# A new order of the work around the first scan of a gated mix of two state space layers

## The chip, the core and the metric

The kernel runs on one core of a Trainium2 chip. The metric is the time of one execution on the device in microseconds (us), and of several executions the median. The engines are named as in the profile: PE is TensorE's matmul, PEld its weight load, DVE is VectorE, ACT is ScalarE, POOL is GpSimd and SP is SyncE. SPq and POOLq are their queues of transfers.

## The reference

Two layers work on the same x (2048 steps, 1024 channels, bf16), and a gate mixes them:

```python
g = sigmoid((x * gate_w).sum(-1, keepdims=True))
# a: a diagonal complex state space layer with 1024 states
Bu = x @ B_bar.T
h[t] = Lam_bar * h[t-1] + Bu[t]
a = 2 * Re(h @ C.T) + x * Dskip
# b: a causal convolution of 2048 taps in each channel, by its spectrum
k_shift = sum(k[t - i] * shift_k[:, i] for i in range(4))
kv = k_shift * v
y = causal_conv(kv, ssm_k) + kv * ssm_D
b = x * y
out = g * a + (1 - g) * b
```

## The kernel before

The work has two stages, and both give TensorE much to do.

**The convolution** goes through eight chunks of 128 channels (`c` from 0 to 7, the loop over `range(NC - 1)` in the lower half of the kernel). For a chunk TensorE makes the four taps of k as products with diagonals (`taps`), the spectrum of the kernel rows (`fwd_K`, PSUM tile `psk`), a mirrored copy (`mirror`), the spectrum of k times v (`fwd_V`, `psv`), and the way back (`inverse`, `psz` and `low`). VectorE multiplies the spectra. `mid_products` is a generator for chunks 1 to 6: it is called piece by piece (`step`) between other work, up to each `yield`. Its products go to `G` and to `T2` (a part of the tile BT[2]), with `WK` and two rotating tiles `t` as rooms; some sums are done by accumulating transfers that POOL issues (`gather`). `overlap` prepares two rows of kernel spectra (`KR`, and the second half of K in place). For even chunks the spectrum of the kernel lies in BT[3], the tile into which the last part of B is loaded after chunk 6. While the loop works on the products of chunk c, it already prepares chunk c + 1 (`n`) and loads c + 2 (`nn`).

**The state space layer** splits time into four blocks `tb` of 512 steps and the states into four groups `g` of 256; 16 pairs (tb, g). `Bu` gives half a pair's product with B at a time (16 matmuls into one PSUM tile `bu`, copied by ScalarE to `U`); these halves are laid out by hand, as fillers, through the convolution and the scans. `scan` treats one pair: the odd steps by VectorE's scan instruction, with turns by a table of sines (`turned`, tiles P and R); the even steps come from the odd ones (`by_lam` on ScalarE makes Q, `evens` adds it to U). `ahead` makes the same for the odd steps (R). `advance(i)` makes `ahead` for one or two later pairs, runs the function `between`, and then scans pair i with the finishing of output row i - 5 (`finish`).

An output row block is 128 steps by 1024 channels. `Cy(tb, tl)` multiplies the states of the four groups by C (32 matmuls, 8 for a group, PSUM tile `psy`), and `scale_a` copies it with the gate to `ga`. `scale_b` scales the convolution's row `pbb` on ScalarE and adds x's skip term by a transfer. `loads` fetches a row of the convolution from DRAM (`cv_scr`, where `inverse` leaves it through `stores`) and one of x; the last four rows (12 to 15) are put into the tiles BT[0] and BT[1], where B's first two groups were. `turn_C` and `part_C` multiply C by complex factors, on VectorE and ScalarE by turns.

What sets the order: every engine takes its instructions in the order in which the Python code issues them (`put` chains them per engine), so the order of the calls is the schedule. PSUM has four tiles of two banks, handed out in rotation (`ps2`): a matmul group waits until the copy of the group four allocations earlier is done. SP issues nearly all loads and stores, in order; POOL issues the accumulating transfers.

Of the kernel before, what the change touches and what calls it, by code (L numbers as in the profile page):

```python
# [9 lines left out]
ALU = mybir.AluOpType  # L10
# [10 lines left out]
def kernel(  # L21
# [40 lines left out]
    NG = NP // 2  # L62
# [29 lines left out]
    def ps2(shape, name):  # L92
        return psum.tile(shape, F32, name=name, tag="ps")
# [17 lines left out]
    def step(gen):  # L111
        next(gen, None)

    def run(gen):
        for _ in gen:
            pass
# [5 lines left out]
    def tt(o, a, b, op):  # L122
        put("dve", V.tensor_tensor, out=o, in0=a, in1=b, op=op)
# [325 lines left out]

    nC = {}  # L450

    def part_C(pi):

        n = nC[pi] = n4([128, 2, D], BF16, "n")
        for c in range(2):
            if pi % 2:
                act(n[:, c], CT[pi][:, 1 - c], func=ACT.Identity, scale=mc2i[:, pi:pi + 1])
            else:
                ts(n[:, c], CT[pi][:, 1 - c], mc2i[:, pi:pi + 1], None, ALU.mult)

    def turn_C(pi):

        if pi % 2 == 0:
            part_C(pi)
        n = nC.pop(pi).rearrange("p c d -> p (c d)")
        for c, f in enumerate((c2r, mc2r)):
            ts(CT[pi][:, c], CT[pi][:, c], f[:, pi:pi + 1], None, ALU.mult)
        o = CT[pi].rearrange("p c d -> p (c d)")
        if pi % 2:
            tt(o, o, n, ALU.add)  # L470
        else:
            gather(o, n)
# [101 lines left out]
    def kr_of(K, h):  # L574

        w = K.shape[3]
        return KR[:, h * 768:h * 768 + 3 * w].rearrange("p (b x) -> p b x", x=w)

    def overlap(c, h=0):

        K = KH[c][h].rearrange("p c b f d -> p c b (f d)")
        tt(kr_of(K, h), K[:, 0, 1:4], K[:, 1, 0:3], ALU.add)
        tt(K[:, 1, 1:4], K[:, 1, 1:4], K[:, 0, 0:3], ALU.subtract)

    def fwd_V(c, fis=range(NFI)):
        eo = eos["v", c]
# [63 lines left out]
    def mid_products(c):  # L650

        GH[c] = spectrum("G", c)
        K, Vt, G = (x[c][0].rearrange("p c b f d -> p c b (f d)") for x in (KH, VH, GH))
        w = 512
        T2 = BT[2].rearrange("p c d q -> p (c d q)")

        def mult(a, k, room):
            t = room.rearrange("p (c b x) -> p c b x", c=2, x=w) if room is not G else G
            ka = kr_of(K, 0)[:, None, a - 1:a] if a and not k else K[:, k:k + 1, a:a + 1]
            tt(t, bc(ka, [128, 2, 4 - a, w]), Vt[:, :, 0:4 - a], ALU.mult)  # L660
            return t

        mult(0, 0, G)
        yield
        gather(G[:, :, 1:], mult(1, 0, WK[:, 0]))
        yield
        t2 = mult(0, 1, T2)
        gather(t2[:, :, 1:], mult(1, 1, WK[:, 1]))
        yield
        i2 = mult(2, 1, u4([128, 4 * w], BF16, "t"))  # L670
        i3 = mult(3, 1, u4([128, 2 * w], BF16, "t"))
        tt(i2[:, :, 1:], i2[:, :, 1:], i3, ALU.add)
        yield
        r2_ = mult(2, 0, WK[:, 0, 0:4 * w])
        r3 = mult(3, 0, WK[:, 0, 4 * w:])
        tt(r2_[:, :, 1:], r2_[:, :, 1:], r3, ALU.add)
        yield
        tt(G[:, :, 2:], G[:, :, 2:], r2_, ALU.add)
        yield
        tt(t2[:, :, 2:], t2[:, :, 2:], i2, ALU.add)  # L680
        tt(G[:, 0], G[:, 0], t2[:, 1], ALU.subtract)
        tt(G[:, 1], G[:, 1], t2[:, 0], ALU.add)

# [75 lines left out]
    def Bu(n=1):  # L759
        steps(Bu_halves, int(2 * n))  # L760
# [131 lines left out]
    def Cy_g(tb, tl, ps, g, last, by_half=False):  # L892
        t0 = HP + tl * 128
        tsl = slice(t0, t0 + 128)
        order = [(j, c, dh) for j in range(2) for c in range(2) for dh in range(2)]
        for j, c, dh in sorted(order, key=lambda o: o[2]) if by_half else order:
            mm(ps[dh], hbs[tb, g][:, c, j, tsl], CT[2 * g + j][:, c, dh * 512:(dh + 1) * 512],
               g == 0 and j == 0 and c == 0, last and j == 1 and c == 1)
# [6 lines left out]
    def scale_a(t_, ps):  # L905
# [2 lines left out]
            act(ga[:, o], i, func=ACT.Identity, scale=gcols[:, t_:t_ + 1])  # L908
        gas[t_] = ga

    def Cy(tb, tl):
        ps = ps2([128, 2, 512], "psy")
        for g in range(NG):
            Cy_g(tb, tl, [ps[:, 0], ps[:, 1]], g, g == NG - 1)
        scale_a(tb * 4 + tl, [(slice(0, D), flat(ps))])

    def finish(t_, ps=None):
# [71 lines left out]
    prod = none  # L989
    for c in range(NC - 1):  # L990
        n, nn = c + 1, c + 2
        if c == 0:
            load("kT", nn)
            load_BT(c, 0)
            load_BT(c, 1)
            load_xT(0)
            load("v", 2)
            load("kn", nn)
            p1 = products(0, 1, by_dma=False)
            step(sp)  # L1000
            fwd_K(n, (0, 1))
            step(p0)
            run(tv)
            overlap(0, 1)
            step(p1)
            step(sp)
            step(p1)
            step(p0)
            step(p1)
            run(p0)  # L1010
            taps(nn, dg)
            load("kT", nn + 1)
            fwd_K(n, (2, 3))
            step(p1)
            step(sp)
            fwd_V(n)
            run(turns)
            dg = dgs(nn + 1)
            run(p1)
            tv = times_v(nn)  # L1020
            step(tv)
            add_skip(nn)
            Bu()
            step(tv)
            taps(nn + 1, dg)
            overlap(n)
            step(sp)
            continue
        tabs, back, last, prod = turn_table(c - 1, u4), inverse(c - 1), prod, mid_products(c)
        if nn + 1 < NC:  # L1030
            load("kT", nn + 1)
        if c == 1:
            load_BT(c, 0)
            load_BT(c, 1)
        if c == 2:
            load_xT(1)
        step(prod)
        run(tv)
        step(prod)
        run(last)  # L1040
        if nn < NC:
            if c > 1:
                taps(nn, dg)
            load("kn", nn)
            tv = times_v(nn)
            step(tv)
        if nn + 1 < NC:
            dg = dgs(nn + 1)
        fwd_K(n)
        if nn + 1 < NC:  # L1050
            load("v", nn + 1)
        store()
        step(prod)
        run(sp)
        step(old)
        step(tabs)
        step(prod)
        if nn < NC:
            add_skip(nn)
            step(tv)  # L1060
        step(back)
        step(back)
        step(prod)
        if n == NC - 1:
            load_BT(3, 0)
            load_BT(3, 1)
        step(tabs)
        step(prod)
        fwd_V(n)
        step(back)  # L1070
        overlap(n)
        if nn < NC:
            run(tv)
        run(back)
        Bu(.5)
        old = tabs

    h3r.close()
    c = NC - 1
# [8 lines left out]
    with tc.tile_pool(name="fin", bufs=1, side="right") as fin:  # L1088
        last, prod, back = prod, products(c, 0, u4, True, fin.tile([128, 4096], BF16, name="t2")), inverse(
            c - 1)  # L1090
        run(last)
        Bu(.5)
        load_BT(2, 0)
        load_BT(2, 1)
        load_xT(2, xt2_pool)
        store()
        ta, tb_ = turn_table(NP - 2, u4), turn_table(NP - 1, u4)
        step(back)
        step(back)
        run(old)  # L1100
        step(ta)
        step(tb_)
        steps(prod, 3)
        step(back)
        ahead(0)
        step(ta)
        step(tb_)
        run(ta)
        run(tb_)
        Bu(.5)  # L1110
        run(back)
        Bu()
        gate(0)
        run(prod)
        load_xT(3)
        ahead(1)
        Bu(2)
        gate(1)
    h3k.close()
    wk = pool("wk", 3, side="right")  # L1120
    wn = pool("wn", 2, side="right")
# [10 lines left out]
    NS = NTB * NG  # L1132
# [6 lines left out]
        scan(i, finish(i - NG - 1) if i > NG else none, mid)  # L1139

    store()
    back = inverse(c)
    step(back)
    step(back)
    advance(0)
    h3.close()

    uh[2] = pool("uh2", UHS[2])
# [3 lines left out]
    for pi in range(4, NP):  # L1152
        load_CT(pi)
    part_C(1)
    Bu()
    turn_C(0)
    advance(1, (lambda: step(back), 1))
# [16 lines left out]
    for k in range(NS - NG):  # L1174
        tb, st = divmod(k, NG)
        if k + 1 < NS - NG:
            loads(k + 1)
        if 6 <= k < 10:
            loads(k + 6)
        store()  # L1180
        if k < NS - 2 * NG:
            advance(k + NG)
            Cy(tb, st)
        elif k + 1 < NS - NG:
            advance(k + NG, between=lambda: [Cy(tb, n) for n in ((st, NG - 1) if st == 2 else (st,))])
        else:
            advance(k + NG)
        if k + 1 < NS - NG:
            scale_b(k + 1)
        if k in (3, 4):  # L1190
            Bu()
        if 7 <= k < 11:
            scale_b(k + 5)
        if tb == 1 and st < 2:
            gate(2 + st)

    store()
    tb = NTB - 1
# [49 lines left out]
```

## Time and profile before

| | |
|---|---|
| median of 3 runs | 406.06 us |
| the three runs | 406.06, 398.39, 410.78 us |
| the profiled execution | 394.97 us |
| its span, first to last instruction | 393.2 us |
| granted TensorE clock, mean | 0.998 |
| busy: PE, DVE, ACT, POOL | 379.2, 368.4, 305.3, 74.1 us |
| share of the 16 DMA engines, queue of SP / queue of POOL | 51.1% / 37.7% |

The busy time of an engine is summed over its instructions. A row of the timeline has start, length, engine, line, operation, output and inputs, and the count of merged instructions; brackets tell how long the engine stood idle ahead of it, and who released it. A row of the waits has who waited for whom, the total in us, how often, and the longest. All compute goes through helpers, so nearly every row says line 100, and the names of the tiles tell the operations apart. In the part on transfers the last number is the median time from issue to landing.

### The profile page before, as it was taken

The page shows a single profiled execution, that of the slowest core. Times are in us where ns is not written, and L with a number is a line of the kernel's source. Part 1 is how long each engine was busy: PE and PEld are TensorE (multiplying, and loading weights), DVE is VectorE, ACT ScalarE, POOL GpSimd, SP SyncE. Part 2 cuts the span into 40 slices and gives each one's busy share as a digit, 9 for nine tenths or more (in the row PEclk, how much of TensorE's full clock was granted, in tenths as well). Part 3 has the DMA queues.
Part 4 walks back from the last instruction along what each step waited for, and adds up shares of the span by engine and source line. Part 5 has one row for each costly group of instructions (what it writes and reads, how often), then busy time and mean ns, then how long its engine had stood idle before and what let it go on. Part 6 is the DMA issues. An engine that isn't in the chain of part 4 may idle for free.

```text
span 393.2 us, 6096 instructions
## 1 busy us (share of the span) xinstructions
PE 379.2 (96%) x2220; PEld 189.2 (48%) x2256; DVE 368.4 (94%) x543; ACT 305.3 (78%) x476; POOL 74.1 (19%) x101
## 2 busy tenths in 40 slices
PE   7999999999999999998999999989999999999995
PEld 3556564646455464443444444434444444444442
DVE  8999997999999999999998699999999999799974
ACT  4897789586878869584983988999789999898521
POOL 3010022221121222210100100100234334334210
PEclk9999999999999999999999999999999999999999
DMA  8979999998978956675999999833579899999644
GB/s 149 175 139 188 236 174 219 213 232 168 195 181 162 239 134 109 144 128 104 178 182 179 222 169 199 208 59 80 109 149 222 169 233 230 244 263 199 136 99 145
DMA packets 132527, 68.44 MB, mean 174 GB/s; under 512 B 114569, under 2 KB 117137, under 8 KB 132498
## 3 DMA queue, kind: packets, MB, share of 16 engines
q1 hardware_dynamic: 120640, 42.22, 51.1%
q0 software_dynamic: 11776, 25.83, 37.7%
q8 instruction: 17, 0.28, 0.3%
q14 instruction: 12, 0.10, 0.1%
q10 hardware_dynamic: 82, 0.02, 0.0%
HBM read 12.87 MB, written 8.39 MB: 54 GB/s over the span
## 4 chain that ended last, share of the span: by engine, by line
DVE 46%; PE 29%; ACT 8%; DMA 8%; issue 5%; SPq 1%; POOL 0%; DVEq 0%; ACTq 0%; POOLq 0%
PE psy L100 19%; DVE wkh L100 9%; DVE G L100 8%; PE bu L100 7%; DVE BT L100 6%; DVE P L100 5%; DVE t L100 3%; DMA G<-wkh 3%; ACT Q L100 3%; DVE R L100 3%; DVE CT L100 2%; DVE ks L100 2%; DMA BT<-in_A_B_im_dram 2%; PE psz L100 2%; DVE U L100 2%
## 5 line engine op out<-in xcount | busy, mean ns | idle before, releaser
L100 PE MATMUL bu<-xT,BT 128*128 128x512 bf16 x496 | 111.9, 379 | 2.2 <-DMA BT<-in_A_B_im_dram 1.4
L100 PE MATMUL psy<-CT,U 128*128 128x512 bf16 x501 | 110.6, 379 | 2.4 <-ACT U L100 1.0
L100 PEld LDWEIGHTS <-U 128*128 128x128 bf16 x512 | 50.0, 98 | 62.0 <-issue 2.2
L100 PEld LDWEIGHTS <-BT 128*128 128x128 bf16 x512 | 49.9, 98 | 61.7 <-DMA BT<-in_A_B_im_dram 1.9
L100 ACT ACTIVATE Q<-U,lam 128x512 bf16<-128x512 bf16 x64 | 37.2, 604 | 18.8 <-DVE U L100 15.2
L100 ACT ACTIVATE U<-bu 128x1024 bf16<-128x1024 f32 x32 | 31.5, 1015 | 10.5 <-PE bu L100 9.6
L100 ACT ACTIVATE R<-U,lam 128x512 bf16<-128x512 bf16 x64 | 37.2, 610 | 0.0
L100 PE MATMUL psk<-kn,KS 128*128 128x512 bf16 x128 | 32.8, 379 | 0.3 <-DVE kn L100 0.3
L100 PE MATMUL psk<-kn,KC 128*128 128x512 bf16 x128 | 32.8, 379 | 0.0
L100 DVE TENSOR_TENSOR_SCAN P<-r,init,P 128x256 bf16<-128x256 f32 x48 | 32.1, 732 | 0.2
L100 DVE TENSOR_TENSOR wkh<-KR,Vh 128x1024 bf16<-128x1024 bf16 (+4 forms) x27 | 29.0, 1100 | 2.6 <-DMA G<-wkh 2.6
L100 PEld LDWEIGHTS <-kT 128*128 128x128 bf16 x512 | 29.4, 98 | 2.8 <-issue 0.8
L100 PE MATMUL taps<-dg,kT 128*128 128x128 bf16 x512 | 30.2, 219 | 0.5 <-DVE dg L100 0.5
L100 ACT ACTIVATE Vh<-psv 128x1024 bf16<-128x1024 f32 x32 | 30.3, 1041 | 0.4 <-PE psv L100 0.4
L100 DVE TENSOR_TENSOR U<-U,Q 128x1024 bf16<-128x1024 bf16 x26 | 17.8, 686 | 7.2 <-ACT Q L100 4.6
L100 ACT ACTIVATE sd<-low 128x1024 bf16<-128x1024 f32 x8 | 8.2, 1020 | 20.2 <-DVE sd L100 20.2
L100 ACT ACTIVATE Kh<-psk 128x1024 bf16<-128x1024 f32 x16 | 16.3, 1022 | 6.3 <-PE psk L100 6.2
L100 ACT ACTIVATE BT<-psk 128x1024 bf16<-128x1024 f32 x16 | 16.1, 1019 | 5.5 <-PE psk L100 5.4
L100 DVE TENSOR_TENSOR R<-TCS,P 128x2048 bf16<-128x2048 bf16 x16 | 19.6, 1225 | 0.5
L100 POOL DMA_DIRECT2D G<-wkh x8 | 9.9, 1236 | 52.5 <-DVE wkh L100 33.7
L100 DVE TENSOR_TENSOR P<-TCS,R 128x2048 bf16<-128x2048 bf16 x16 | 19.5, 1220 | 0.3
L100 PEld LDWEIGHTS <-KC 128*128 128x128 bf16 x128 | 12.5, 98 | 15.1 <-ACT KC L100 0.3
(166 smaller groups left out, 651.5 us busy)
## 6 DMA issues: line engine op xcount, KB each, us to landing
G<-wkh POOLq DMA_DIRECT2D x7, 768.0 KB, 7.2
BT<-wkh POOLq DMA_DIRECT2D x6, 768.0 KB, 8.0
cv_scr<-sd SPq DMA_DIRECT2D x8, 512.0 KB, 3.5
pbb<-cv_scr SPq DMA_DIRECT2D x12, 256.0 KB, 3.8
xr<-in_A_x_dram SPq DMA_DIRECT2D x12, 256.0 KB, 4.8
pbb<-gd POOLq DMA_DIRECT2D x12, 256.0 KB, 4.2
v<-in_B_v_dram SPq DMA_DIRECT2D x5, 512.0 KB, 5.3
R<-R POOLq DMA_DIRECT2D x10, 256.0 KB, 4.8
```

Of the source, the lines that this page charges most:

```text
L100: i = f(*a, **kw)
```

## The change

Nothing is computed differently; five orders change.

- In `mid_products` the sum of the third mirror products is put behind the next product, the last products' sum gets a step of its own, and so does the last sum into T2. In the loop the last sums of G come behind the multiplication by v of the chunk after next, and the first half of `overlap` stands ahead of a sum.
- `inverse` of the last chunk: its first products stand ahead of the last of four half products with B and ahead of the loads of C, `gate(1)` comes later, and that half product stands behind the first scan.
- The output rows (2, 0) and (2, 1) are begun together: the products of three groups for both, then the last group of the first; the last group of (2, 1) with row (2, 2) one scan later.
- The loads of rows 12 to 15 are issued in the passes 0 to 3 of the last loop, not in 6 to 9.
- One half product with B moves from pass 4 to pass 5, and `scale_b` of rows 10 and 14 from the end of pass 9 to the middle of pass 10.

`N_BY_ACT` and `C_BY_DMA` name the same parts of C as the parity did before.

```diff
-            if pi % 2:
+            if pi in N_BY_ACT:
...
-    def overlap(c, h=0):
+    def overlap(c, h=0, parts=(0, 1)):
...
-        tt(kr_of(K, h), K[:, 0, 1:4], K[:, 1, 0:3], ALU.add)
-        tt(K[:, 1, 1:4], K[:, 1, 1:4], K[:, 0, 0:3], ALU.subtract)
+        if 0 in parts:
+            tt(kr_of(K, h), K[:, 0, 1:4], K[:, 1, 0:3], ALU.add)
+        if 1 in parts:
+            tt(K[:, 1, 1:4], K[:, 1, 1:4], K[:, 0, 0:3], ALU.subtract)
...
         i2 = mult(2, 1, u4([128, 4 * w], BF16, "t"))
         i3 = mult(3, 1, u4([128, 2 * w], BF16, "t"))
+        yield
+        r2_ = mult(2, 0, WK[:, 0, 0:4 * w])
         tt(i2[:, :, 1:], i2[:, :, 1:], i3, ALU.add)
-        yield
-        r2_ = mult(2, 0, WK[:, 0, 0:4 * w])
         r3 = mult(3, 0, WK[:, 0, 4 * w:])
+        yield
         tt(r2_[:, :, 1:], r2_[:, :, 1:], r3, ALU.add)
         yield
         tt(G[:, :, 2:], G[:, :, 2:], r2_, ALU.add)
         yield
         tt(t2[:, :, 2:], t2[:, :, 2:], i2, ALU.add)
+        yield
         tt(G[:, 0], G[:, 0], t2[:, 1], ALU.subtract)
...
+    begun = {}
+
+    def Cy_begin(tb, tl):
+        ps = begun[tb, tl] = ps2([128, 2, 512], "psy")
+        for g in range(NG - 1):
+            Cy_g(tb, tl, [ps[:, 0], ps[:, 1]], g, False)
+
     def Cy(tb, tl):
-        ps = ps2([128, 2, 512], "psy")
-        for g in range(NG):
-            Cy_g(tb, tl, [ps[:, 0], ps[:, 1]], g, g == NG - 1)
+        if (tb, tl) not in begun:
+            Cy_begin(tb, tl)
+        ps = begun.pop((tb, tl))
+        Cy_g(tb, tl, [ps[:, 0], ps[:, 1]], NG - 1, True)
...
         step(prod)
-        run(last)
+        step(last)
         if nn < NC:
             if c > 1:
                 taps(nn, dg)
             load("kn", nn)
             tv = times_v(nn)
             step(tv)
+        run(last)
...
         step(tabs)
         step(prod)
+        overlap(n, 0, (0,))
+        step(prod)
         fwd_V(n)
         step(back)
-        overlap(n)
+        overlap(n, 0, (1,))
...
         load_xT(3)
         ahead(1)
-        Bu(2)
-        gate(1)
+        Bu(1.5)
+        back = inverse(c)
+        step(back)
+        step(back)
...
     store()
-    back = inverse(c)
-    step(back)
-    step(back)
     advance(0)
+    Bu(2 - 1.5)
...
     part_C(1)
+    gate(1)
     Bu()
...
-        if 6 <= k < 10:
-            loads(k + 6)
+        if k < 4:
+            loads(k + 12)
...
-            advance(k + NG, between=lambda: [Cy(tb, n) for n in ((st, NG - 1) if st == 2 else (st,))])
+            def rows():
+                if st == 0:
+                    Cy_begin(tb, 0)
+                    Cy_begin(tb, 1)
+                for n in ((0,), (1, 2), (3,))[st]:
+                    Cy(tb, n)
+                if st == 2:
+                    scale_b(k)
+                    scale_b(k + 4)
+
+            advance(k + NG, between=rows)
...
-        if k + 1 < NS - NG:
+        if k + 1 < NS - NG and k != 9:
             scale_b(k + 1)
-        if k in (3, 4):
-            Bu()
-        if 7 <= k < 11:
+        Bu({3: 1, 4: .5, 5: .5}.get(k, 0))
+        if 7 <= k < 11 and k != 9:
             scale_b(k + 5)
```

More of the change, by code (lines that the diff above doesn't have):

```diff
@@ L450 @@
     nC = {}
+    N_BY_ACT = (1,3,5,7)
+    C_BY_DMA = (0,2,4,6)
     def part_C(pi):
@@ L461, in turn_C @@
     def turn_C(pi):
-        if pi % 2 == 0:
+        if pi not in nC:
             part_C(pi)
@@ L468, in turn_C @@
         o = CT[pi].rearrange("p c d -> p (c d)")
-        if pi % 2:
+        if pi not in C_BY_DMA:
             tt(o, o, n, ALU.add)
@@ L671, in mid_products @@
         i3 = mult(3, 1, u4([128, 2 * w], BF16, "t"))
-        tt(i2[:, :, 1:], i2[:, :, 1:], i3, ALU.add)
         yield
         r2_ = mult(2, 0, WK[:, 0, 0:4 * w])
+        tt(i2[:, :, 1:], i2[:, :, 1:], i3, ALU.add)
         r3 = mult(3, 0, WK[:, 0, 4 * w:])
+        yield
         tt(r2_[:, :, 1:], r2_[:, :, 1:], r3, ALU.add)
```

## The prediction

> **What bounds the kernel now.** I read the busy times first, then the table by stretches, then the waits of TensorE and of VectorE, and last the timeline around each moved step.
>
> ```profile
> PE 379.2 (96%) x2220; PEld 189.2 (48%) x2256; DVE 368.4 (94%) x543; ACT 305.3 (78%) x476; POOL 74.1 (19%) x101
> ```
> ```profile
> 75.29:97.42 22.13, 22.02 (x151) 11.98 (x151) 21.99 (x21) 17.45 (x25) 4.28 (x5) 1.00 1.05 211
> ```
> ```profile
> 260.00:312.00 52.00, 49.84 (x255) 23.17 (x260) 51.25 (x94) 47.68 (x88) 13.85 (x16) 1.00 0.70 142
> 312.00:361.00 49.00, 48.79 (x252) 22.64 (x256) 46.06 (x82) 44.35 (x85) 17.26 (x20) 1.00 1.07 235
> 361.00:388.50 27.50, 27.28 (x125) 12.25 (x125) 22.60 (x36) 12.22 (x20) 6.04 (x7) 1.00 0.57 128
> ```
> ```profile
> PE bu L100 <- DMA BT<-in_A_B_im_dram: 1.4, 1, 1.4
> ...
> PE psy L100 <- ACT U L100: 1.0, 1, 1.0
> PE psy L100 <- ACT ga L100: 0.9, 1, 0.9
> ...
> PE low L100 <- ACT sd L100: 0.7, 1, 0.7
> ```
>
> The first row has TensorE at 96% and VectorE at 94%: two engines nearly full. The stretches tell them apart. The first number is the length, then busy time of PE, weight loads, DVE, ACT, POOL, the clock, the DMA share and GB/s. The row of 22.13 us is one chunk of the convolution, cut from the start of its first kernel product to that of the next chunk: TensorE has 22.02 us of work in it, so its gaps are 0.11 us. From 361 to 388.5 us it is just as full, with 125 recorded matmuls in 27.5 us, about 0.22 us each. The waits list all that TensorE loses once it has started: 1.4 + 1.0 + 0.9 + 0.7 = 4.0 us. The change leaves the number of matmuls as it is. It can therefore win at most those 4.0 us, about 1% of the span, unless the pace of TensorE itself were changed. It can lose much more, since any engine that comes late stops TensorE.
>
> **The sums of the convolution.** In each of six chunks the products are split into one more step. The kernel rows' first overlap, the second mirror product and the multiplication by v are put between sums that feed each other.
>
> ```profile
> 78.00 2.36 DVE L100 TENSOR_TENSOR G<-G,BT 128x2048 bf16<-128x2048 bf16 x2
> 80.28 1.22 DVE L100 TENSOR_TENSOR ks<-ks,v 128x2048 bf16<-128x2048 bf16 x1
> ...
> 85.28 1.82 DVE L100 TENSOR_TENSOR t<-BT,Vh 128x2048 bf16<-128x2048 bf16 x2
> 87.14 0.69 DVE L100 TENSOR_TENSOR t<-t 128x1024 bf16<-128x1024 bf16 x1
> 87.75 1.82 DVE L100 TENSOR_TENSOR wkh<-KR,Vh 128x2048 bf16<-128x2048 bf16 x2
> ```
> ```profile
> 82.19 0.38 PE L100 MATMUL mirror<-ks,refl 128*128 128x512 bf16 x1
> 82.62 1.03 PE L100 MATMUL psz<-G,CI 128*128 128x512 bf16 x4
> 83.49 1.03 PE L100 MATMUL psz<-G,SI 128*128 128x512 bf16 x4
> ```
>
> The sum t<-t needs the product ahead of it: it starts at 87.14, 0.04 us after that ended (85.28 + 1.82). The product behind it needs nothing of it and starts at 87.75, 0.08 us before t<-t ends. A dependent neighbour thus costs 0.12 us. Four such pairs in a chunk are parted (this one, the sum in wkh, the two halves of the overlap, and the last t2 sum with the G sums behind it): 4 x 0.12 x 6 = 2.9 us of VectorE. [...] The trace shows the 0.12 us at this pair, and I go by it.
>
> TensorE hides nearly all of this. Its margins here even grow: now ks<-ks,v ends at 81.50 and the mirror product starts at 82.19, 0.69 us later. After the change ks is done 2.3 us earlier (the two sums take 2.36) and the final sums end at about 81.5; the first inverse product reads only the first of them, done by 80.3 (margin 2.3), and the second starts at 83.49 (margin 2.0). So I see no new wait there. One thing speaks against it: the product r2 writes a buffer that the transfer G<-wkh still reads, and it now stands ahead of a sum of 0.69 us. Where that transfer is late, the sum waits too.
>
> ```profile
> DVE wkh L100 <- DMA G<-wkh: 2.6, 1, 2.6
> ```
>
> It was late once in the kernel before, so I take 0.7 us off what VectorE gains, and nothing off the time.
>
> ```profile
> 142.36 1.22 DVE L100 TENSOR_TENSOR BT<-BT,t 128x2048 bf16<-128x2048 bf16 x1
> ```
> ```profile
> 141.89 1.02 ACT L100 ACTIVATE ks<-taps 128x1024 bf16<-128x1024 f32 x1 [0.43 <-PE taps L100]
> ```
> ```profile
> 173.61 7.99 DMA BT<-in_A_B_im_dram
> ```
>
> What can come through is the wait for the last half of B. It is loaded at 173.61, when VectorE has finished the last product that reads the same tile, and takes 7.99 us; TensorE waits 1.4 us for it. VectorE's lead at that point: 4 x 0.12 in each of the four chunks up to the fifth, less 0.7, is 1.2 us. But in the last chunk with taps ks can't start before ScalarE's copy ends at 142.91, and with the lead it would come at 142.36 + 1.14 - 1.2 = 142.3. That holds the lead to 0.6; the pairs behind it give back 0.2 to 0.3. I take **0.8 us**, between 0 (the lead is all held) and 1.4 (all of the wait).
>
> **Inverse's last products ahead of a half product.**
>
> ```profile
> 199.74 13.97 PE L100 MATMUL bu<-xT,BT 128*128 128x512 bf16 x62
> 213.55 0.94 PE L100 MATMUL p<-gwb,xT 128*128 128x1 bf16 x32
> ```
> ```profile
> 217.80 7.07 PE L100 MATMUL bu<-xT,BT 128*128 128x512 bf16 x31
> 218.00 1.02 ACT L100 ACTIVATE sd<-psz 128x1024 bf16<-128x1024 f32 x1 [0.70 <-PE psz L100]
> 218.93 0.71 ACT L100 ACTIVATE Q<-U,lam 128x512 bf16<-128x512 bf16 x1
> ...
> 221.08 0.69 DVE L100 TENSOR_TENSOR U<-U,Q 128x1024 bf16<-128x1024 bf16 x1 [2.33 <-ACT Q L100]
> ...
> 223.95 0.49 DVE L100 TENSOR_SCALAR CT<-CT,c2r 128x1024 bf16<-128x1024 bf16 x1 [0.91 <-ACT n L100]
> ```
>
> TensorE has four half products (13.8 us, 3.45 each), the gate (0.8) and then 16 inverse products (3.45) whose copy ends at about 218.9; only then does ScalarE begin Q. After the change the inverse products stand one half product and one gate earlier, 4.25 us. ScalarE begins Q at about 214.7, the wait of 2.33 goes, and so does most of 0.91, since n follows Q with one copy between: VectorE gains 3.2 us. The moved gate(1) costs its 0.8 us of TensorE in either place, and its two small ScalarE operations stand behind n. No transfer stands ahead of the moved steps that was not there.
>
> VectorE and ScalarE run almost without a gap from here on, so both keep these 3 us. TensorE has a store of half products to do and isn't waiting for them. What comes through is the wait for ScalarE's U copies: 0.97 us.
>
> ```profile
> 260.28 3.74 ACT L100 ACTIVATE U<-bu 128x1024 bf16<-128x1024 f32 x4
> ```
>
> The first of four copies starts at 260.28 and frees the PSUM that the first output row needs. ScalarE 3 us earlier frees it at about 258, ahead of TensorE's last product. I take **1.0 us**; bounds 0 and 1.0.
>
> **Half a product moved.** After output row (1,0) TensorE did two half products and a gate, so that row (1,1) took the PSUM tile of row (1,0) itself:
>
> ```profile
> 302.64 1.91 ACT L100 ACTIVATE U<-bu 128x1024 bf16<-128x1024 f32 x2
> ...
> 310.36 1.09 ACT L100 ACTIVATE ga<-psy,gcols 128x1024 bf16<-128x1024 f32 x1
> ```
>
> TensorE was through with it at about 310.5 (the copy's first release at 311.45, less the wait of 0.9). With one half there, row (1,1) falls on the tile of the half product before, whose copy ended at 304.55, and the next half product on row (1,0)'s tile at about 314, after 311.45. I take **0.9 us**; bounds 0 and 0.9.
>
> **Rows begun, loads, scale_b.** Begun rows reorder TensorE's work alone: the last group of row (2,0) comes 24 matmuls (5.2 us) later, and two of four PSUM tiles are held, which the next rows don't need. The copy of row (2,0) may start only 5.2 us later too, but ScalarE runs behind by more: row (1,0) ended two half products and a gate (7.7 us) before 310.5, and its copy began at 310.36. Cost 0, covered by that lateness; without the cover 5.2 us of ScalarE, less the 5.3 us of slack shown below. The last four pairs of loads need B's first two tiles, free when TensorE ends at 260.4. On SP's queue they block the load for row 2, which is asked for by scale_b(2):
>
> ```profile
> 245.48 0.43 SPq L100 DMA_DIRECT2D pbb<-cv_scr  x1
> ```
> ```profile
> 283.99 1.14 ACT L100 ACTIVATE pbb<-pbb,omg 128x1024 bf16<-128x1024 bf16 x1
> ```
>
> It moves from 245.5 to about 261 and has until 284. Cost 0. The later stores wait for at most another 1 to 2 us of SP. Between 312 and 361 the loads leave a stretch at DMA share 1.07 for one at 0.70. scale_b(10) moves one scan later, and its transfer has about 5 us until finish(10) reads it; if VectorE waits 2 to 3 us there, the end hides it:
>
> ```profile
> 375.52 0.76 DVE L100 TENSOR_TENSOR U<-R 128x512 bf16<-128x512 bf16 x2
> ...
> 378.54 1.49 DVE L100 TENSOR_TENSOR U<-U,Q 128x1024 bf16<-128x1024 bf16 x2 [2.26 <-ACT Q L100]
> ```
>
> TensorE's last 32 matmuls start at 388.5 - 32 x 0.216 = 381.6, and the last odd rows are done at 376.3: 5.3 us of slack.
>
> **The sum.** 0.8 + 1.0 + 0.9 = 2.7 us, bounds 0 and 4.0 (with the wait for sd, which I leave). Against the profiled execution of 394.97 us (span 393.2 and 1.8 around it) that is 392.3. The median of the three runs, 406.06, is 11 us above that execution and I can't see where those are spent; I take the gain off the median: **403.4 us**, and 402.1 to 406.1 for this case alone.
>
> **Rivals.** (1) *VectorE is the real bound*, and all that it gains falls out. The row of weight loads (48%) speaks for it. Its gains would be 3.2 (first scan), 2.9 (pairs) and the wait for the transfers Q<-Q, which lie where DMA is relieved:
>
> ```profile
> DVE U L100 <- DMA Q<-Q: 2.5, 2, 2.1
> ```
>
> 8.6 us, so 397.5. [...] Against it: in no stretch do matmuls come faster than in the full ones. I give it 0.18, also for the 11 us that I can't place. (2) *Slower: the moved loads slow the gathers.* The gathers behind scale_b are just in time in this stretch:
>
> ```profile
> DVE xr L100 <- DMA pbb<-gd: 0.2, 1, 0.2
> ```
> ```profile
> pbb<-cv_scr SPq DMA_DIRECT2D x12, 256.0 KB, 3.8
> ...
> pbb<-gd POOLq DMA_DIRECT2D x12, 256.0 KB, 4.2
> ...
> BT<-cv_scr SPq DMA_DIRECT2D x4, 256.0 KB, 8.3
> ```
>
> Equal loads took 3.8 us in the free stretch and 8.3 in the full one. If pbb<-gd grew by those 4.5 us in three scans, VectorE would lose 13.5, and beyond the 5.3 of slack the end comes 8.2 later: 414.3. It decides as soon as a gather lands later than before, since one was 0.2 us late already. Against it: the share there is 0.70. Chance 0.10. (3) *Nothing comes through*: each wait returns at the next PSUM tile or at the next late load, 406.1. Chance 0.16.
>
> **The numbers.** Forecast 0.56, the rivals 0.18, 0.10 and 0.16. A measurement of this kernel can tell about 2% (8.1 us) from no change: faster than 397.9 is rival 1, 0.18; slower than 414.2 is rival 2, 0.10; the rest, 0.72, lies between. The range is from 396.2 (rival 1 with the 1.3 us between my sum and its upper bound) to 409.2 (no change, and a quarter of the 12.4 us by which the three runs differ, 398.39 to 410.78); rival 2 stays outside.
>
> **What would show it.** Right: TensorE's waits list without psy<-ACT U and psy<-ACT ga and with less than 1.4 us for BT; VectorE's wait for Q near 221 gone; the first U<-U,Q 3 us earlier; chunks still 22.1 us long. Wrong: chunks shorter than 22.0 us (VectorE was the bound), a wait of psz for G, xr waiting for pbb<-gd by microseconds, or an output row waiting for PSUM.

## The result, and the profile after

| | before | after |
|---|---|---|
| median of 22 runs each, side by side | 398.74 us | 393.42 us |
| lowest and highest | 394.43, 416.94 us | 391.44, 408.53 us |
| runs above 400 us | 8 | 3 |
| the profiled execution, its span | 394.97, 393.2 us | 392.88, 390.9 us |

The 22 runs of before include the three that were known when the forecast was made. The ratio of after to before is 0.9917, with a 95% interval of 0.9888 to 0.9947; it leaves out executions that were disturbed on the way, so none of the gain is owed to these becoming rarer. The gain is real and small: 0.83% of 398.74 us is 3.3 us, 2.1 to 4.5 by the interval, and under the 2% that the prediction counts as no change. The forecast was a gain of 2.7 us, but it put the time at 403.4 us and the range's lower end at 396.2 us.

After's busy times, then its waits of TensorE (who waited for whom, us in total, times, longest):

```profile
PE 380.4 (97%) x2220; PEld 190.2 (49%) x2256; DVE 367.0 (94%) x543; ACT 306.1 (78%) x476; POOL 74.3 (19%) x101
```
```profile
PE low L100 <- ACT sd L100: 0.7, 1, 0.7
...
PE bu L100 <- DMA BT<-in_A_B_im_dram: 0.5, 1, 0.5
```

Of the three waits of before that were aimed at, the two of psy are gone and that for BT has gone from 1.4 to 0.5; the fourth, that for sd, stands as it was. That is 0.9 + 1.0 + 0.9 = 2.8 us. The spans of the two profiled executions differ by a little less, 2.3 us. What TensorE does between its waits hasn't changed, as after's table by stretches shows (length; busy time of PE, weight loads, DVE, ACT, POOL; clock, DMA share, GB/s):

```profile
76.13:98.26 22.13, 22.02 (x151) 11.96 (x151) 20.86 (x21) 17.42 (x24) 3.67 (x5) 1.00 1.10 202
```
```profile
260.00:312.00 52.00, 51.68 (x265) 24.03 (x270) 48.81 (x87) 45.26 (x85) 13.80 (x16) 1.00 0.85 179
312.00:361.00 49.00, 48.74 (x252) 22.61 (x255) 48.31 (x86) 46.25 (x87) 17.64 (x20) 1.00 0.97 197
```

A chunk still takes 22.13 us with 22.02 of TensorE's work in it, although VectorE is now idle for 1.3 us of it. Between 260 and 312 us TensorE works 51.68 us where it worked 49.84; this is where the psy waits lay. The share of the transfers has become even, 0.85 and 0.97 for 0.70 and 1.07.

The first scan, and the copies that freed PSUM too late, in after's timelines of ScalarE and VectorE:

```profile
214.72 0.71 ACT L100 ACTIVATE Q<-U,lam 128x512 bf16<-128x512 bf16 x1
...
257.68 3.73 ACT L100 ACTIVATE U<-bu 128x1024 bf16<-128x1024 f32 x4
```
```profile
216.89 0.69 DVE L100 TENSOR_TENSOR U<-U,Q 128x1024 bf16<-128x1024 bf16 x1
...
220.66 0.49 DVE L100 TENSOR_SCALAR CT<-CT,c2r 128x1024 bf16<-128x1024 bf16 x1 [1.82 <-ACT n L100]
...
290.09 0.69 DVE L100 TENSOR_TENSOR xr<-xr,pbb 128x1024 bf16<-128x1024 bf16 x1 [2.33 <-DMA pbb<-gd]
...
376.15 1.49 DVE L100 TENSOR_TENSOR U<-U,Q 128x1024 bf16<-128x1024 bf16 x2 [2.26 <-ACT Q L100]
```

Q begins at 214.72 (218.93 before), the first sum with it at 216.89 (221.08), the turn of C at 220.66 (223.95), the copies of U at 257.68 (260.28). So ScalarE was ahead by 4.2 us and by 2.6 us when it counted. The last row, near the end of the kernel, keeps its wait of 2.26 us for Q. One wait was not there before: xr waits 2.33 us for the gather pbb<-gd, to be taken up below. TensorE's output rows began with a wait in before:

```profile
261.35 27.79 PE L100 MATMUL psy<-CT,U 128*128 128x512 bf16 x125 [0.97 <-ACT U L100]
...
311.50 7.07 PE L100 MATMUL psy<-CT,U 128*128 128x512 bf16 x31 [0.87 <-ACT ga L100]
```

In after they start with none, so their rows have no bracket:

```profile
260.16 27.79 PE L100 MATMUL psy<-CT,U 128*128 128x512 bf16 x125
...
305.86 7.07 PE L100 MATMUL psy<-CT,U 128*128 128x512 bf16 x31
```

### The profile page after: what moved, and what is told of

Read it like the earlier page. It is cut to its first block, busy times and chain, and to the rows that moved or that the text cites. A ratio compares the mean times of both kernels' runs of the same rounds, so it can differ in the third digit from the quotient of the medians.

```text
span 390.9 us, 6094 instructions
## 1 busy us (share of the span) xinstructions
PE 380.4 (97%) x2220; PEld 190.2 (49%) x2256; DVE 367.0 (94%) x543; ACT 306.1 (78%) x476; POOL 74.3 (19%) x101
## 4 chain that ended last, share of the span: by engine, by line
PE 55%; DVE 20%; issue 11%; DMA 5%; ACT 4%; POOL 3%; DVEq 0%; POOLq 0%
PE bu L100 14%; PE psk L100 11%; PE psy L100 9%; PE taps L100 7%; PE psz L100 6%; PE psv L100 6%; DVE P L100 5%; DMA pbb<-gd 3%; DVE R L100 2%; DMA BT<-in_A_B_im_dram 2%; DVE CT L100 2%; DVE U L100 2%; POOL ga L100 2%; DVE BT L100 1%; PE low L100 1%
## 5 line engine op out<-in xcount | busy, mean ns | idle before, releaser
L100 PEld LDWEIGHTS <-kT 128*128 128x128 bf16 x512 | 30.6, 101 | 2.9 <-issue 1.1
L100 PE MATMUL taps<-dg,kT 128*128 128x128 bf16 x512 | 31.4, 224 | 0.3 <-DVE dg L100 0.3
L100 PE MATMUL psv<-ks,SF 128*128 128x512 bf16 x64 | 19.0, 379 | 0.6 <-DVE ks L100 0.5
```

The costliest lines, as they stand in the source:

```text
L100: i = f(*a, **kw)
```

## The experiments

The theory: TensorE is the bound, and each part of the change is worth the wait of TensorE that it takes away. The rivals were the prediction's own, and one that the result added: that the change moves the late and irregular transfers of the first half, so that the high executions become rarer. Each ratio is to the kernel before, run on the same chip at the same time.

### The parts one by one

**e1_sums**, and once more as **b2_sums_again**: the new order in `mid_products`, `overlap` and the loop over chunks alone, that is, the pieces of the change from `overlap` to the G sum and those in the loop. The core of it:

```diff
-        tt(i2[:, :, 1:], i2[:, :, 1:], i3, ALU.add)
         yield
         r2_ = mult(2, 0, WK[:, 0, 0:4 * w])
+        tt(i2[:, :, 1:], i2[:, :, 1:], i3, ALU.add)
```

> The kernel before with the new order of the convolution's sums alone. Theory (TensorE is the bound; what comes through is a wait of TensorE that goes): TensorE's wait for the last half of B falls from 1.4 us to about 0.5, the waits psy<-ACT U and psy<-ACT ga stay, chunks stay 22.1 us long, and the time falls by 0.9 us (ratio to before 0.998). Rival (VectorE is the bound): the 2.6 to 2.9 us that VectorE saves come through, chunks are about 21.7 us, ratio 0.993.

> The kernel before with the new order of the sums alone, a second time, for more runs. Theory: undisturbed runs 0.9 us below those of before, ratio 0.998. Rival on the scatter (the order of the sums takes it away): at most one in five of its runs is over 400 us, where half of those of before are.

Measured: 0.9983 (0.9869 to 1.0097), then with twice the runs 0.9989 (0.9950 to 1.0029), medians 403.57 and 397.83 us. The waits of b2_sums_again, in part:

```profile
PE psy L100 <- ACT U L100: 1.0, 1, 1.0
...
PE psy L100 <- ACT ga L100: 0.9, 1, 0.9
...
PE bu L100 <- DMA BT<-in_A_B_im_dram: 0.4, 1, 0.4
```

The wait for BT falls to 0.4 and the two waits of psy stay, as expected. This execution has two waits that before's profile doesn't have, 1.6 us (psk <- ACT sd) and 0.9 us (psk <- kn). In time the part gives 0.1%, less than the interval can tell.

**b1_no_sums**: the changed kernel with this part undone, the hunk above reversed.

```diff
+        tt(i2[:, :, 1:], i2[:, :, 1:], i3, ALU.add)
         yield
         r2_ = mult(2, 0, WK[:, 0, 0:4 * w])
-        tt(i2[:, :, 1:], i2[:, :, 1:], i3, ALU.add)
...
```

> The changed kernel without the new order of the sums (inverse, half product, rows and loads are kept). Theory (TensorE is the bound, the waits add up): TensorE's wait for the last half of B is back at about 1.4 us, the waits psy<-ACT U and psy<-ACT ga stay away; 0.9 us more than the changed kernel, ratio to before about 0.993. Rival on the scatter (the order of the sums, 50 to 170 us into the run, takes the scatter away): the runs scatter like those of the kernel before, half of them over 400 us; if the scatter is taken away by something else, or by chance, one in five is.

Measured: 0.9942 (0.9901 to 0.9982), 393.91 us. The wait for BT is back at 1.5 us, both psy waits stay away:

```profile
PE bu L100 <- DMA BT<-in_A_B_im_dram: 1.5, 1, 1.5
```

So the later parts carry most of the gain. The changed kernel's 0.9917 lies 0.0025 lower, 1.0 us, the size of the wait; but the two intervals overlap.

The wait for BT isn't tied to this part alone. Two kernels with the old order of the sums, both taken up below, c3_rows_only and b4_before_vsum, show in this order

```profile
PE bu L100 <- DMA BT<-in_A_B_im_dram: 0.9, 1, 0.9
PE bu L100 <- DMA BT<-in_A_B_im_dram: 0.2, 1, 0.2
```

With the old sums the wait for BT goes with VectorE's wait for G<-wkh: 0.2 beside 0.4 us (b4_before_vsum), 0.9 beside 0.9 (c3_rows_only), 1.1 beside 1.2 (e4_rows_loads), 1.5 beside 1.9 (b1_no_sums), 1.4 beside 2.6 and 2.8 (before, c2_loads_only). With the parted sums and no other edit on VectorE it is 0.4 to 0.5 in seven profiles, and 1.4 in e6_low. So the parted sums lower it, but how much of the 0.9 us is theirs depends on how late that transfer is.

**e2_inverse**: only inverse's last products, `gate(1)` and the half product beside them.

```diff
-        Bu(2)
-        gate(1)
+        Bu(1.5)
+        back = inverse(c)
+        step(back)
+        step(back)
...
```

> The kernel before with the new order of inverse's last products and the gate alone. Theory: VectorE's wait for Q of 2.3 us near 221 goes, its first U<-U,Q comes about 3 us earlier, TensorE's wait psy<-ACT U (1.0 us) goes, BT and psy<-ACT ga stay; time -1.0 us (ratio 0.9975). Rival (VectorE is the bound): -3.2 us, ratio 0.992.

Measured: 400.86 us median, 394.11 to 412.12, too scattered on this chip for an interval (the kernel before had 395.47 to 436.37 beside it). The trace tells more than the time. TensorE's timeline of e2_inverse around the output rows:

```profile
257.68 11.39 PE L100 MATMUL bu<-xT,BT 128*128 128x512 bf16 x51
268.90 6.42 PE L100 MATMUL psy<-CT,U 128*128 128x512 bf16 x28
```
```profile
303.44 7.07 PE L100 MATMUL psy<-CT,U 128*128 128x512 bf16 x32
310.34 7.07 PE L100 MATMUL bu<-xT,BT 128*128 128x512 bf16 x31
317.25 0.94 PE L100 MATMUL p<-gwb,xT 128*128 128x1 bf16 x32
318.05 4.26 PE L100 MATMUL psy<-CT,U 128*128 128x512 bf16 x18
```

Neither row of psy has a bracket: this one part takes away the wait for U, as expected, and also the wait for ga, which was expected to stay. ScalarE comes earlier to both: it begins the copies of U 2.5 us before TensorE is ready for its row, where it was 0.1 us in before, and the copy of ga 1.5 us before, where it was 0.3. TensorE was held up by 5.9 us near 149 us in this execution; but e1_sums, held up by 13.9, shows both psy waits at 1.0 and 0.9, so a hold-up doesn't remove them. The wait for BT, expected to stay, isn't there either; it is missing in e3_half too, and both were held up ahead of it, so neither tells anything of BT.

**e3_half**: only the half product moved from pass 4 to pass 5.

```diff
-        if k in (3, 4):
-            Bu()
+        Bu({3: 1, 4: .5, 5: .5}.get(k, 0))
```

> The kernel before with half a product with B moved by one pass and nothing else. Theory: the wait psy<-ACT ga (0.9 us) goes and nothing else; time -0.9 us (ratio 0.998). Rival (VectorE is the bound): nothing on VectorE changes, ratio 1.000.

Measured: 1.0053 (0.9902 to 1.0205), 400.75 us. The wait for ga is gone, that for U stays at 1.0, as expected; the interval says nothing of the time.

**e4_rows_loads**: begun rows, earlier loads, later `scale_b`. Then each alone: **c2_loads_only** (the hunk of `loads`) and **c3_rows_only** (the rest).

```diff
-        if 6 <= k < 10:
-            loads(k + 6)
+        if k < 4:
+            loads(k + 12)
...
```

> The kernel before with the rest of the change: rows begun together, the last four pairs of loads earlier, two scale_b later. Theory: none of TensorE's waits changes, ratio 1.000 within 0.001; VectorE's wait for Q<-Q (2.5 us) shrinks without worth. Rival (VectorE is the bound): -2.5 us, ratio 0.994. Second rival (the scatter of the kernel before comes from transfers in the full stretch of the last loop): the five runs lie closer together than those of the kernel before, and their median falls by several us.

> The kernel before with the four pairs of loads moved to passes 0 to 3 and nothing else. Theory (the loads delay the gather behind scale_b(2), and without the 3 us that the new order of inverse gives to VectorE the delay reaches TensorE by ScalarE's copies): VectorE waits 2.0 us for pbb<-gd near 291, TensorE's waits for ACT ga rise from 0.9 to 2.8 us, ratio to before 1.004 to 1.005. Rival (the begun rows make these waits): waits as in the kernel before, ratio 1.000.

> The kernel before with the two rows begun together and the two scale_b later, and nothing else. Theory: TensorE's waits stay as in the kernel before, 0.9 us for ACT ga, ratio 1.000 within 0.001. Rival (the begun rows make the waits for ACT ga): 2.8 us for ACT ga, ratio 1.005.

Measured: e4_rows_loads 1.0019 (0.9932 to 1.0106); c2_loads_only **1.0060 (1.0018 to 1.0102)**, 400.49 us; c3_rows_only 0.9983 (0.9944 to 1.0022), 396.57 us. In e4_rows_loads TensorE's waits were expected to stay as they were; it waits 1.9 us for ga ahead of an output row and 0.9 ahead of a half product. The two parts taken alone say where the first comes from; the second shows in neither. The begun rows leave the waits of psy as they were, 1.0 and 1.0, and cost nothing that their interval can tell, as forecast. The loads do cost, and c2_loads_only shows how. Its chain of waits, its timelines of VectorE, ScalarE and TensorE, in this order:

```profile
285.22 5.89 DMA pbb<-gd
```
```profile
291.14 0.69 DVE L100 TENSOR_TENSOR xr<-xr,pbb 128x1024 bf16<-128x1024 bf16 x1 [0.96 <-DMA pbb<-gd]
```
```profile
298.62 0.72 ACT L100 ACTIVATE Q<-U,lam 128x512 bf16<-128x512 bf16 x1 [1.51 <-DVE U L100]
...
311.21 1.09 ACT L100 ACTIVATE ga<-psy,gcols 128x1024 bf16<-128x1024 f32 x1
```
```profile
304.76 4.91 PE L100 MATMUL bu<-xT,BT 128*128 128x512 bf16 x22
309.51 0.94 PE L100 MATMUL p<-gwb,xT 128*128 128x1 bf16 x32
312.36 8.75 PE L100 MATMUL psy<-CT,U 128*128 128x512 bf16 x32 [1.91 <-ACT ga L100]
```

The gather lands 5.89 us after its issue, where the same one took 4.7 in before. VectorE waits 0.96 for it, ScalarE waits for VectorE's U, its copy of the output row starts at 311.21 instead of 310.36, and TensorE waits 1.91 us for the copy instead of 0.87. The path is the expected one; both waits are smaller than expected (2.0 and 2.8 us). Then 32 matmuls take 8.75 us, where 31 took 7.07 in before (the row at 311.50 above). The clock in the stretches of c2_loads_only says why (the clock is the number ahead of the last two):

```profile
305.00:312.30 7.30, 5.45 (x54) 2.91 (x53) 7.20 (x14) 7.27 (x16) 2.44 (x3) 1.00 0.94 192
312.36:314.20 1.84, 1.84 (x6) 0.67 (x6) 1.84 (x4) 1.84 (x3) 0.66 (x2) 0.58 0.97 166
314.20:316.20 2.00, 2.00 (x7) 0.74 (x5) 1.97 (x4) 2.00 (x7) 0.29 (x1) 0.53 0.80 138
316.20:321.00 4.80, 4.80 (x25) 2.21 (x24) 4.73 (x10) 4.77 (x12) 1.74 (x2) 1.00 1.00 220
```

After the wait TensorE was granted 0.58 and 0.53 of its clock for 3.8 us. So the wait cost its own 1.0 us more and another 1.5 to 1.7 (8.75 less 7.07, with or without a matmul of 0.2 for the one more), 2.5 to 2.7 us together; the ratio gives 0.006 x 397.8 = 2.4 us.

**c1_loads_back**: the changed kernel with the loads in passes 6 to 9 again (the hunk above reversed).

> The changed kernel with the last four pairs of loads where they were before, in passes 6 to 9. Theory: the gather pbb<-gd lands in time again, so VectorE's wait of 2.3 us near 290 goes and VectorE ends some 2 us earlier; TensorE is the bound and hides it, so undisturbed runs equal the changed kernel's within 0.3 us (ratio 0.989 to 0.992). Rival (the moved loads bring part of the gain): +1 us or more, a wait of TensorE or of VectorE for transfers returns between 320 and 350. Rival (the moved loads cost time): 1 us faster than the changed kernel.

Measured: 0.9916 (0.9874 to 0.9957), the changed kernel's 0.9917 again. The moved loads that cost 2.4 us alone cost nothing measurable beside the other parts. In the changed kernel the same gather takes longer still, in after's chain of waits:

```profile
282.80 7.27 DMA pbb<-gd
```

It takes 7.27 us (4.7 before) and VectorE waits 2.33. But TensorE has no wait behind it. VectorE and ScalarE are ahead by the earlier inverse (the gather is issued at 282.80 instead of 285.42), and that lead can cover the wait; the half product that moved can too, since it changes which copy the output row waits for. No run parts the two. The moved loads bring nothing measurable.

### Is TensorE the bound?

**a0_all** is the changed kernel, unedited, beside the next three. **e7_pe** adds 16 matmuls to it, by doing the first 8 of the 16 matmuls of two half products twice into the same PSUM tile, in the first scans:

```diff
-            for c in range(2):
+            for c in (0, 0, 1) if i == 8 else range(2):
```

**e8_dve** adds VectorE work instead, the first third of the overlap once more in each of six chunks, 0.42 us each:

```diff
         overlap(n, 0, (0,))
+        K = KH[n][0].rearrange("p c b f d -> p c b (f d)")
+        tt(kr_of(K, 0)[:, 0], K[:, 0, 1], K[:, 1, 0], ALU.add)
```

**e6_low** looks for the wait that was left, low <- ACT sd of chunk 6, and puts a half product between `psz` and `low`:

```diff
         steps(prod, 3)
+        Bu(.5)
         step(back)
...
-        Bu(.5)
         run(back)
```

> The changed kernel as it is, as the base of the three beside it. Ratio to before 0.992. Theory on the scatter (late transfers between 50 and 100 us stop VectorE and TensorE in some executions, in any order of the later work): its runs scatter as widely as those of the kernel before on this chip, 10 us and more. Rival (the change takes the scatter away): its runs lie within 3 us.

> The changed kernel with 16 matmuls more (the first half of two half products with B of group (2,0) is done twice, so that it is computed again with the same result): 16 x 0.216 = 3.45 us of TensorE between the first and the second scan, nothing on VectorE. Theory (TensorE is the bound): +3.45 us against the changed kernel, ratio to before 1.000 to 1.001. Rival (VectorE is the bound): +0 to 0.5 us, ratio 0.992.

> The changed kernel with one VectorE operation more in each of six chunks (a third of the overlap row is computed a second time, 128x512, about 0.42 us): 2.5 us of VectorE, nothing on TensorE. Theory (TensorE is the bound, VectorE has 0.6 to 0.7 us of slack in a chunk of 22.14): +0 us, at most the 0.9 us won at the last half of B; chunks stay 22.1. Rival (VectorE is the bound): +2.5 us, ratio to before 0.998.

> The changed kernel with one half product with B put between psz and low of chunk 6, where TensorE waits 0.68 us for the copy sd. Theory (TensorE is the bound): that wait goes, 0.7 us less than the changed kernel, ratio to before 0.990; VectorE's sum of sd comes 3.5 us later and costs nothing. Rival (VectorE is the bound): no change against the changed kernel, or slower by what VectorE then waits.

Measured: a0_all 0.9889 (0.9851 to 0.9927), 393.55 us. e7_pe 1.0000 (0.9960 to 1.0041), 397.41 us: 3.9 us above a0_all by the medians, 3.3 by the lowest times (395.32 and 392.06), and 4.4 by the two ratios, whose intervals lie apart. Added were 16 x 0.216 = 3.45 us. TensorE's work comes out in the time about one for one.

e8_dve has only six executions, 393.64 and 393.66 us and four between 403.76 and 421.17; its interval, 0.9797 to 1.0000, doesn't tell the two expectations apart. The two low ones stand at a0_all's median although 2.5 us of VectorE were added, which speaks for the theory without settling it: its lowest time lies 1.6 us above a0_all's.

e6_low 0.9890 (0.9840 to 0.9940), 394.18 us: in its profile low no longer waits for sd, but the wait for BT is at 1.4 instead of a0_all's 0.4, and there are two that a0_all doesn't have, psk <- ACT sd with 1.8 us and psz <- DVE G with 0.7. The profiled execution, 396.89 us, lies 2.7 us above the median. Where the 0.7 us went isn't shown by it; no gain can be measured. **c4_low_loads_back**, e6_low with the loads of c1_loads_back, was tried as a version better than both:

> The changed kernel with the loads where they were before and one half product between psz and low of chunk 6. Theory: TensorE's wait for sd (0.7 us) goes and VectorE's for pbb<-gd too; 0.7 us less than the changed kernel, ratio to before 0.987 to 0.990. Rival (VectorE's later sum of sd costs as much): equal to the changed kernel.

Measured: 0.9942 (0.9897 to 0.9987), 396.81 us, where 0.987 to 0.990 was expected. No version beat the changed kernel.

### Where the time above 400 us comes from

Both kernels have single executions far above their lowest time. e1_sums was profiled in one of them (span 409.3 us). Its waits of TensorE, of VectorE, and a row of its chain of waits:

```profile
PE psk L100 <- DMA kn<-in_B_ssm_D_dram: 13.9, 2, 11.9
```
```profile
DVE wkh L100 <- DMA G<-wkh: 13.3, 1, 13.3
```
```profile
54.40 21.87 DMA G<-wkh
```

The same transfer in the chains of before and of e3_half (span 416.2 us):

```profile
53.98 11.87 DMA G<-wkh
```
```profile
54.35 25.75 DMA G<-wkh
```

An accumulating transfer of the first chunks takes 21.87 and 25.75 us instead of 11.87. VectorE waits for it. In e1_sums TensorE waits for the row of `kn` that POOL issues; in e3_half it waits 5.7 us for that row and 13.4 for a copy of ScalarE that stands behind the late transfer in the chain. The other executions above 408 us that were profiled show the same two names: e8_dve (span 419.3) two waits for `kn`, the longer 17.1 us, and 6.4 in all for G; c4_low_loads_back (414.8) two for `kn`, 13.0 together, and two for G, 11.0 together. Both wait for other transfers as well, VectorE for BT<-wkh 9.0 us in e8_dve and 7.1 in c4_low_loads_back. None of the four is an execution of before itself. To move the scatter with that one transfer: **b3_vsum** is the changed kernel with chunk 1's first sum into G on VectorE, **b4_before_vsum** the kernel before with the same edit.

```diff
-        gather(G[:, :, 1:], mult(1, 0, WK[:, 0]))
+        n1 = mult(1, 0, WK[:, 0])
+        if c == 1:
+            tt(G[:, :, 1:], G[:, :, 1:], n1, ALU.add)
+        else:
+            gather(G[:, :, 1:], n1)
```

> The changed kernel with the first sum of G in chunk 1 on VectorE in place of an accumulating transfer of 768 KB (1.75 us of VectorE more, no wait for G<-wkh there, which was 0.6 to 16.5 us in the profiles so far). Theory (TensorE is the bound; the scatter comes from transfers that are late between 50 and 100 us): undisturbed runs equal the changed kernel's within 0.3 us, ratio 0.989 to 0.992, and fewer runs are over 400 us. Rival (VectorE is the bound): +1.75 us less the wait. Second rival (the scatter comes from other transfers, such as the transposed loads of the kernel rows): as many runs over 400 us as the changed kernel has.

> The kernel before with that one sum on VectorE and nothing else. Theory: undisturbed runs equal those of before (ratio 1.000 within 0.002), since VectorE's wait of 2.6 us there was hidden behind TensorE; if the late transfer G<-wkh makes the scatter, clearly fewer than half of the runs are over 400 us. Second rival (other transfers make it): half of them still are.

Measured: 0.9934 (0.9897 to 0.9972) and 1.0005 (0.9969 to 1.0040); 3 of 12 executions above 400 us in each. High executions come without that transfer too, so it isn't their only cause. Over the result and the last three sessions the kernel before is above 400 us in 47 of 116 executions; the changed kernel and its near variants (a0_all, b1_no_sums, b3_vsum, c1_loads_back, c4_low_loads_back, e6_low) in 15 of 89. In the first session it was 9 of 11 for the kernel before. But the mark of 400 us stands 3.3 us further above the changed kernel's usual time than above before's. At 396.7 us, the mark lowered by these 3.3 us, 26 of the 89 lie above, and against 47 of 116 that is no longer a clear difference. So it isn't shown that the change makes late transfers rarer.

## Why the prediction was right or wrong

- **The step that failed: "I take the gain off the median".** The three runs had a median of 406.06 us; 22 runs of the same kernel, these three among them, had 398.74. The level was 7.3 us too high, nearly three times the gain. The prediction had seen that the median stood 11 us above the profiled execution and couldn't say where they were spent. In the four profiled executions above 408 us, all of edited kernels, such time is spent behind late transfers of the convolution; that it was so in the two high runs of the three is likely and not shown. Four executions of ten of this kernel lie above 400 us, and of the three runs two did. Off the profiled execution the same sum gave 392.3, and the profiled execution of after took 392.88. The range failed by the same step: its lower end, 396.2, was counted from 406.06 too. The level is 7.3 us of the whole miss of 10.0 (403.4 against 393.42). The rest is that the medians fell by 5.3 us where 2.7 was forecast; the ratio gives 3.3 of these 5.3 to the change, and the other 2 go with fewer high runs of after, which may be chance.
- **TensorE is the bound: right.** Chunks of 22.13 us as before, and 3.45 us of matmuls added 3.3 to 4.4.
- **BT, 0.8 forecast: 0.9 in the trace (1.4 to 0.5), the size in part by luck.** The parted sums lower the wait (e1_sums, b1_no_sums), but with the old sums it stands anywhere between 0.2 and 1.5, with the lateness of G<-wkh. From c3_rows_only's 0.9 the same end would have been a gain of 0.4. The price of a dependent neighbour holds in kind: VectorE is busy for 366.7 to 367.2 us in six profiles with the parted sums and no other VectorE edit (after, a0_all, e1_sums, e7_pe, e6_low, b2_sums_again), and for 368.4 to 369.0 in five with the old ones (before, e2_inverse, e3_half, e4_rows_loads, b1_no_sums), by the means 1.6 us less by 24 pairs. Forecast were 2.9; of a pair's 0.12 us the busy time can show only the 0.08 of overlap, 1.9 in all. The hold on the lead was seen too: VectorE's wait for ScalarE's ks is 1.1 us in each of the seven profiles with the old sums, and in after

```profile
DVE ks L100 <- ACT ks L100: 3.4, 5, 1.2
```

  so what the pairs save can be waited away there. The parted sums' other profiles have 1.1 to 4.8 us in this wait. In time the part gives 0.1 to 0.3%, which no interval here tells from nothing.
- **U, 1.0: right, by the cause forecast** (e2_inverse has it, e1_sums and e3_half don't). "Most of 0.91" was wrong: the wait for n grew to 1.82, because VectorE reached it 4.2 us earlier and n came 3.3 us earlier. The lead behind it, 3.3 us, agrees with the 3.2 forecast.
- **ga, 0.9: right in size, the cause half right.** The half product removes it (e3_half), but the earlier inverse alone removes it too (e2_inverse). The two terms don't add up by their parts; the sum came out because each wait was counted once.
- **Begun rows, cost 0: right** within what c3_rows_only can tell. **Loads, cost 0: wrong as it stood.** Alone they cost 0.6%. Rival 2's mechanism is there, 2.6 us on one gather (4.7 to 7.3), and the prediction had set against it only that the DMA share was 0.70. Its sign of being wrong, xr waiting for pbb<-gd by microseconds, did show, with 2.33 us. What keeps it from TensorE is another part of the change: the lead by the earlier inverse, which the prediction had put down as a gain of its own, or the moved half product.
- **Rival 1** (VectorE the bound) falls by the chunks and e7_pe. The row of weight loads (48%) that the prediction let speak for it told nothing of room: weight loads are busy for 49% of after, and yet 16 matmuls more, 3.45 us of TensorE, came out as 3.3 to 4.4 us of time. **Rival 3** falls by the interval, 0.9888 to 0.9947.

## What to carry to other kernels

Where two engines are almost full, cut out one repeated stage and compare its length with each engine's work in it, then add up the waits of the fuller one: as long as its own pace stays the same, a reordering can win no more than that sum. Here 2.8 us of the 4.0 went, and the time fell by 3.3 with an interval of 2.1 to 4.5. Take such a gain off the profiled execution or off the lowest times; a median of three runs that lies 11 us above the profiled execution is a question about those runs first. And a part that is free only beside another part has to be written down with that condition, since here it costs 0.6% when it stands alone.

## What was not expected of the hardware

TensorE's granted clock fell to about half behind a short pause. In c2_loads_only 1.91 us of idle time, behind 0.9 us of products one column wide, were followed by a granted clock of 0.58 and 0.53 for 3.8 us; in e4_rows_loads 1.90 us at the same place by 0.64 in the stretch from 313 to 317 us. In the kernel before 0.87 us at this place left the clock at 1.00. A longer pause was followed by the same pace in c1_loads_back's timeline of TensorE, where four matmuls take 1.89 us behind 5.21 us of idle time and 1.03 a little later:

```profile
104.08 1.89 PE L100 MATMUL psk<-kn,KS 128*128 128x512 bf16 x4 [5.21 <-DMA kn<-in_B_ssm_D_dram]
105.76 1.82 PE L100 MATMUL psk<-kn,KC 128*128 128x512 bf16 x4
107.42 1.03 PE L100 MATMUL psk<-kn,KS 128*128 128x512 bf16 x4
```

Not every pause of this size did it, and not always at once. e6_low's and b3_vsum's timelines of TensorE, in this order:

```profile
144.92 1.02 PE L100 MATMUL psk<-kn,KS 128*128 128x512 bf16 x4 [1.79 <-ACT sd L100]
```
```profile
145.74 1.04 PE L100 MATMUL psk<-kn,KS 128*128 128x512 bf16 x4 [3.03 <-DMA kn<-in_B_ssm_D_dram]
146.61 1.72 PE L100 MATMUL psk<-kn,KC 128*128 128x512 bf16 x4
```

Behind a pause of 1.79 us four matmuls took 1.02, and the mean granted clock of that whole execution is 1.000. Behind one of 3.03 us the first four matmuls still ran at full pace, 1.04 us, and the next four took 1.72. Whether the narrow products ahead of the pause in c2_loads_only and e4_rows_loads count as part of it, or the moment at which the pause falls decides, is not shown.

The slow pace lasted 3.8 us in c2_loads_only and 3.3 in c1_loads_back. So a wait of 1.91 us cost nearly twice itself, the 1.5 to 1.7 us of slower matmuls added, where behind the one of 0.87 us the clock stayed at 1.00: the price of a wait didn't grow in proportion here.
